# Half of the block sums of g moved from GpSimd instructions to adding DMAs, the first x in four loads, and a new written-out order

## The chip, the cores and the metric

The kernel runs on one core of a Trainium2 chip. The metric is the device time of one execution in microseconds (us). The kernel before takes 213.96 us, the median of three runs (213.93 to 214.35). Profiles come from one execution; its engines are TensorE (PE, with its weight loads listed apart as PEld), VectorE (DVE), ScalarE (ACT), GpSimd (POOL) and SyncE (SP, which here only issues DMAs). A queue named with a q (SPq, POOLq) is the sequencer of that engine.

## What is computed

Eight batches `b` of 8 heads, 512 tokens and 32 state rows, each of 64 elements. Tokens and state rows attend to each other, both with one shared score matrix, and the result goes through a two-layer network with a leaky rectifier:

```python
def _attn_ref(x, state):
    scores = scale * np.matmul(x, state.transpose(0, 1, 3, 2))
    a = softmax(scores)                      # over the 32 state rows
    xread = np.matmul(a, state)
    scores2 = scale * np.matmul(state, x.transpose(0, 1, 3, 2))
    a2 = softmax(scores2)                    # over the 512 tokens
    sread = np.matmul(a2, x)
    return np.concatenate([xread, sread], axis=2)

def _moe_ref(x, w_in, w_out, alpha):         # 4352 rows of 512; d_ff = 2048
    h = x @ w_in
    g = np.maximum(h, 0.0) + alpha * np.minimum(h, 0.0)
    return g @ w_out
```

## The kernel before

Every instruction is written out by hand in one string, `ORDER` (L18 to L99). A loop (L767) reads it token by token and calls the step that the token names, so the string fixes the order of the instructions on every engine and on every DMA queue. Each engine then works through its own instructions strictly in order, and waits where an operand is not there yet.

**The stages.** Since xread is `a @ state`, the first layer for the token rows is `a @ (state @ w_in)`. Steps `m` and `mo` make `m = state @ w_in` for batch b and quarter f of d_ff (PE, then a copy out of PSUM by ACT or DVE). The softmax over states is made by `sc` (scores, PE), `sb` (a 32 x 32 block transpose, DVE), `smax` (DVE), `ssh` (subtract, mostly POOL), `sexp` (ACT), `ssum` (DVE), `snorm` (multiply, POOL or DVE, L405) and `wb` (transpose back, DVE). Batch 0 takes a path of its own with smaller tiles: `cx` casts the loaded x, `xt` transposes it on PE, `xo` copies it out, `tsc` makes the scores, `at` and `ao` turn the weights. The softmax over tokens is `tm`, `nb`, `te`, `tsum`, `tn` and two DMA transposes (`xd` for x, `tt` for the weights); `rd` multiplies it with x on PE. The state rows of all batches are gathered and run through the network as a ninth, half-wide batch, b = 8.

**First layer.** `F.b.jc.k` is two matmuls of 512 columns (L556; four of 256 columns for b = 8, L565) into PSUM bank k, for one 128-row slice jc of d_ff. `N.b.jc` (ACT, L609) takes the negative part, `G.b.jc` (DVE, L612) adds it, times 1 - alpha, to h and writes the f16 tile g. `f`, `n` and `g` do the same for half of the tokens of batch 0.

**Second layer.** Batch 0 uses plain matmuls (`S`, L626). Batches 1 to 8 use a scheme with seven products of half-size blocks in place of eight. It needs four sums of blocks of w_out, made once (`W`, L670), and for each batch four sums of blocks of g (`U.b.i.c.e`, L683 to L694; i is the sum, c one half of it, e the engine). A block of g is (half of the tokens, half of d_ff), and all 64 sums are POOL instructions of 128 x 1024 f16 (128 x 512 for b = 8). Sum 2 reads sum 1, and sum 4 reads sum 2. `P.b.p.i.c` is product p: four matmuls of 256 columns (L715). Products 5, 6, 7 and 3 read sums 1, 2, 3 and 4. `K` copies a running product out of PSUM (L731), `Q` writes a quarter of the output: a sum or a copy into an `oq` tile, of which there are four, and a store issued by SP (L749).

**Loads.** The x of batch 0 comes in two loads of SP as f32 (L170) and is cast by DVE. All other loads (x of later batches L160, the states L203, w_in L212, w_out L218) are issued by POOL, which casts in the DMA. `Z.k.n` is a run of n idle matmuls that fill a wait of PE (L236). The small vector alpha comes in four loads of SP (L188) and is turned by `oma`.

Of the kernel before, what the change touches and what calls it, by code (L numbers as in the profile page):

```python
# [13 lines left out]
ALU = mybir.AluOpType  # L14
# [4 lines left out]
Z.0.3 stc.a stt.0 cx.0.1.v xt.0.0.1.1 xo.0.0.1.a wi.0 cx.0.0.v xt.0.0.0.2 xo.0.0.0.a sbd.0.v lst sbd.1.v Z.3.2 sto.a  # L19
Z.3.2 Z.3.3 cx.1.0.v xt.0.1.0.3 cx.1.1.v tsc.0.1.4 tsc.0.0 smax.0.0 ssh.v.0.0 xo.0.1.0.a xt.0.1.1.5 xo.0.1.1.a Z.1.3  # L20
Z.1.2 sc.0.0 sc.0.1 tsc.1.1.1 m.0.0.2.0 tsc.1.0 sexp.0.0 tm.0 smax.0.1 ssum.0.0 Z.3.3 mo.0.0.a.1 lx.1 Z.3.2 Z.3.2
Z.3.3 ssh.v.0.1 str.1.3 nb.0.a te.0.1 Z.5.3 str.0.5 Z.4.3 Z.4.3 te.0.0 sexp.0.1 Z.4.2 mo.0.0.v.0 Z.4.3 wi.1 ssum.0.1
wo.0 sro.0.a xt.1.0.0.4 snorm.p.0.0 at.0.0 ao.0.a wo.1 Z.1.3 tsum.0 snorm.p.0.1 xt.1.0.1.1 m.1.0 xt.1.1.0.2 sro.1.a
wi.2 oma.a xo.1.0.0.v wi.3 xo.1.0.1.v xo.1.1.0.a f.0.0.0.5 xt.1.1.1.0 n.0.0.0 mo.1.0.v at.1.4 ao.1.v m.0.1.1.3
tn.0.1.p mo.0.1.v.1 m.1.1 mo.1.1.a g.0.0.0.0 g.0.0.0.1 f.0.0.1.2 n.0.0.1 f.0.1.1.4 mo.0.1.a.0 n.0.1.1 f.0.1.0.3
xo.1.1.1.v g.0.0.1.1 g.0.0.1.0 sc.1 tm.1 m.2.0.5.0 mo.2.0.a.1 mo.2.0.a.0 F.0.5.1 N.0.5 F.0.4.2 N.0.4 nb.1.a te.1.1
g.0.1.1.0 g.0.1.1.1 G.0.5 S.0.3.0.0 wo.2 G.0.4 S.0.1.0.5 S.0.1.1 sb.1 F.0.7.4 N.0.7 G.0.7 F.0.6.1 wo.3 tn.0.0.p N.0.6
S.0.3.1 G.0.6 n.0.1.0 g.0.1.0.0 S.0.2.2.2 S.0.3.2 te.1.0 S.0.1.2 S.0.2.0 g.0.1.0.1 m.0.2 S.0.2.3 S.0.1.3 smax.1
mo.0.2.a F.0.8.4 N.0.8 G.0.8 W.1.1.p F.0.11.1 N.0.11 G.0.11 tsum.1 F.0.10.3 N.0.10 m.0.3 mo.0.3.a W.1.0.p lx.2 S.0.2.1
S.0.3.3 F.0.9.4 m.1.2 F.0.12.1 ssh.p.1 sexp.1 G.0.10 S.0.2.5 S.0.1.5 ssum.1.s N.0.9 G.0.9 F.0.13.3 S.0.3.5 mo.1.2.a  # L30
# [769 lines left out]
```

## Time and profile before

| What | us |
|---|---|
| median of three runs | 213.96 |
| the profiled execution | 214.07 |
| its span, first to last instruction | 212.0 |
| PE busy | 203.3 |
| POOL busy | 179.1 |
| DVE busy | 174.2 |
| ACT busy | 152.6 |
| the 64 sums of g on POOL (four groups of 16) | 128.0 |
| idle matmuls (L236) | 10.5 |

The profiled execution took 2.07 us more than its span; that part lies outside the instructions. Busy times overlap across engines. A PE that is busy all the time is one whose matmuls follow each other without a gap; the time from one matmul's start to the next is what it costs there, and less than the duration listed for one matmul, since matmuls are pipelined. The granted TensorE clock is full throughout.

### The profile page before, as it was taken

How to read it: one execution, taken by the hardware profiler on the slowest of the kernel's cores; microseconds unless marked ns; L12 is line 12 of the kernel's file. 1: busy time of each engine (PE TensorE's matmuls, PEld its weight loads, DVE VectorE, ACT ScalarE, POOL GpSimd, SP SyncE). 2: the span in 40 equal slices, each digit the busy share in tenths (PEclk: the TensorE clock that was granted, in tenths of full speed). 3: DMA queues.
4: the chain of work that ended last, by engine and by line, in shares of the span. 5: the costliest groups of instructions: out<-in, count | busy, mean ns of one | idle time of the engine just before them, and what ended most of it. 6: DMA issues, size and time to landing. Idle time of an engine off the chain costs nothing.

```text
span 212.0 us, 5108 instructions
## 1 busy us (share of the span) xinstructions
PE 203.3 (96%) x2034; PEld 137.7 (65%) x2034; DVE 174.2 (82%) x260; ACT 152.6 (72%) x300; POOL 179.1 (84%) x111
## 2 busy tenths in 40 slices
PE   7899999999999999999999998999999999999991
PEld 4556333444666665677667875667688777888880
DVE  0787988999999999999999999898999777654340
ACT  2577979999999999999797777887954584234100
POOL 8048848998999899999996999479996999999860
PEclk9999999999999999999999999999999999999999
DMA  6999995966665436778744539011521201111232
GB/s 159 219 204 207 206 204 89 160 165 90 152 105 89 106 84 135 110 134 143 183 117 49 103 106 192 3 51 40 162 53 49 99 3 49 49 53 49 74 124 102
DMA packets 43975, 23.70 MB, mean 112 GB/s; under 512 B 22192, under 2 KB 43440, under 8 KB 43952
## 3 DMA queue, kind: packets, MB, share of 16 engines
q1 hardware_dynamic: 31904, 15.22, 27.9%
q0 software_dynamic: 11776, 8.09, 26.6%
q8 instruction: 16, 0.26, 0.5%
q10 hardware_dynamic: 272, 0.07, 0.1%
q14 instruction: 7, 0.06, 0.1%
HBM read 17.31 MB, written 8.91 MB: 124 GB/s over the span
## 4 chain that ended last, share of the span: by engine, by line
PE 88%; DMA 7%; ACT 2%; issue 1%; SPq 0%; DVE 0%; ACTq 0%
PE h L556 25%; PE px L715 23%; PE pv L715 12%; PE o L626 6%; PE py L715 5%; PE m_ps L507 4%; PE h L565 3%; PE fill L236 3%; DMA xT<-xg 2%; DMA x<-in_x_dram 2%; PE sr_ps L480 2%; DMA out_dram<-oq 2%; DMA e2T<-e 1%; PE sc L314 1%; PE xT_ps L299 1%; PE h L578 1%
## 5 line engine op out<-in xcount | busy, mean ns | idle before, releaser
L612 DVE SCALAR_TENSOR_TENSOR g<-neg,oma_sb,h 128x512 f16<-128x512 f32 (+1 forms) x140 | 92.7, 708 | 11.6 <-ACT neg L609 11.1
L609 ACT ACTIVATE neg<-h 128x512 f32<-128x512 f32 (+1 forms) x140 | 75.0, 585 | 23.0 <-PE h L556 14.4
L556 PE MATMUL h<-aT,m 128*128 128x512 f16 x248 | 67.2, 379 | 0.1
L715 PEld LDWEIGHTS <-gsum 128*128 128x128 f16 x480 | 46.1, 98 | 16.8 <-issue 1.8
L715 PEld LDWEIGHTS <-g 128*128 128x128 f16 x360 | 35.0, 98 | 9.1 <-issue 0.9
L694 POOL TENSOR_TENSOR gsum<-g 128x1024 f16<-128x1024 f16 (+1 forms) x16 | 32.0, 2009 | 4.2 <-DVE g L612 3.6
L694 POOL TENSOR_TENSOR gsum<-g,g 128x1024 f16<-128x1024 f16 (+1 forms) x16 | 32.0, 2004 | 3.9 <-DVE g L612 3.8
L556 PEld LDWEIGHTS <-m 128*128 128x128 f16 x248 | 23.7, 98 | 15.5 <-issue 0.8
L694 POOL TENSOR_TENSOR gsum<-gsum,g 128x1024 f16<-128x1024 f16 (+1 forms) x16 | 32.1, 2006 | 1.1
L715 PE MATMUL px<-ws,gsum 128*128 128x256 f16 x240 | 32.6, 273 | 0.0
L694 POOL TENSOR_TENSOR gsum<-g,gsum 128x1024 f16<-128x1024 f16 (+1 forms) x16 | 31.9, 2005 | 0.1
L731 ACT COPY kept<-px 128x512 f32<-128x512 f32 (+1 forms) x22 | 12.7, 577 | 14.0 <-PE px L715 13.7
L533 ACT CAST m<-m_ps 128x512 f16<-128x512 f32 x36 | 20.0, 613 | 1.8 <-PE m_ps L507 1.5
L384 POOL TENSOR_TENSOR ts<-ts,mx 128x1024 f32<-128x1024 f32 x7 | 13.4, 1908 | 5.4 <-DVE mx L379 5.4
L715 PE MATMUL px<-w_out_sb,gsum 128*128 128x256 f16 x120 | 17.4, 273 | 0.0
L715 PE MATMUL pv<-ws,gsum 128*128 128x256 f16 x120 | 17.2, 273 | 0.0
L748 DVE TENSOR_TENSOR oq<-pv,kept 128x512 f32<-128x512 f32 (+1 forms) x16 | 10.5, 655 | 8.1 <-PE pv L715 6.7
L626 PE MATMUL o<-w_out_sb,g 128*128 128x512 f16 x64 | 17.1, 380 | 0.0
L715 PE MATMUL pv<-ws,g 128*128 128x256 f16 x120 | 16.9, 273 | 0.0
L715 PE MATMUL px<-w_out_sb,g 128*128 128x256 f16 x120 | 16.9, 273 | 0.0
L715 PE MATMUL py<-w_out_sb,g 128*128 128x256 f16 x120 | 16.2, 273 | 0.0
L531 ACT CAST m<-m_ps 128x1024 f16<-128x1024 f32 x12 | 12.4, 1032 | 1.3 <-PE m_ps L507 1.2
(76 smaller groups left out, 251.6 us busy)
## 6 DMA issues: line engine op xcount, KB each, us to landing
out_dram<-oq SPq DMA_DIRECT2D x28, 256.0 KB, 2.5
xg<-in_x_dram POOLq DMA_DIRECT2D x7, 512.0 KB, 6.9
w_in_sb<-in_moe_w_in_dram POOLq DMA_DIRECT2D x4, 512.0 KB, 9.3
w_out_sb<-in_moe_w_out_dram POOLq DMA_DIRECT2D x4, 512.0 KB, 12.2
x<-in_x_dram SPq DMA_DIRECT2D x2, 512.0 KB, 5.3
out_dram<-osb SPq DMA_DIRECT2D x4, 256.0 KB, 2.2
out_dram<-oq SPq DMA_DIRECT2D x4, 128.0 KB, 2.1
st<-in_state_dram POOLq DMA_DIRECT2D x1, 224.0 KB, 8.0
```

The source lines that it names most:

```text
L384: engine(e).tensor_tensor(blocks(cols(live["ts", b], j, S)), blocks(scored(b, j)), over_blocks(cols(live["mx", b], j, S // N)), ALU.subtract,)
L507: nc.tensor.matmul(t[N * k : N * (k + 1), :], st_head(b, h)[64 * r : 64 * r + 64, :], w_in_sb[64 * r : 64 * r + 64, c, 512 * f : 512 * (f ...
L531: copier(e)(m_tile(b, f), t)
L533: copier(e)(m_tile(b, f)[:, g, :], t[g])
L556: nc.tensor.matmul(h.rearrange("p (r j s) -> p r j s", r=2, j=2), ms[b, f][:, g, 128 * j : 128 * (j + 1)], weights(b, g), start=(g == 0), ...
L609: nc.scalar.activation(neg, h, RELU, bias=0.0, scale=-1.0)
L612: nc.vector.scalar_tensor_tensor(g_tile(b, jc), negs.pop((b, jc)), oma_sb[:, jc : jc + 1], hs.pop((b, jc)), ALU.mult, ALU.add,)
L626: nc.tensor.matmul(outs[b, q], g_tile(b, jc)[:, 128 * q : 128 * (q + 1)], w_out_sb[:, jc, :], start=not begun and jc == 2 * jc2, stop=left ...
L694: engine(e).tensor_tensor(t, x(), y(), op)
L715: nc.tensor.matmul(pbanks[b, name][:, i, :], of(b, c)[:, j, 128 * i : 128 * (i + 1)], moving[:, 4 * c + j, :], start=not begun and j == 0, ...
L731: copier(e)(t, pbanks[b, "x"])
L748: nc.vector.tensor_tensor(osb, pbanks[b, name], kept[b, add], ALU.add)
```

## The change

1. **Sums 3 and 4 of g** (`U.b.3` and `U.b.4`, 32 of the 64) carry the letter `d`: no POOL arithmetic, but a DMA issued by POOL that reads one block and adds it to another in place. Sum 3 then lies in the block (second half of the tokens, first half of d_ff), sum 4 in the block (first half of the tokens, second half of d_ff), and products 7 and 3 read them there. All four sums are plain additions now.
2. **Signs.** The sums of w_out's blocks are formed with other signs, and the kept products 2 and 4 are stored times -1.
3. **The first x** comes in four loads of half the size: two issued by SP, two by ACT, behind the load of the first states. The states of batches 1 to 7 come in two loads (`lst.0`, `lst.1`). The loads of alpha became a step (`la`) behind a memset on POOL; the memset of `st_pairs` went from DVE to POOL.
4. **The order** is written anew throughout, with engines chosen anew: of the six normalisations of states on DVE all are now on POOL, and more copies out of PSUM are on DVE and fewer on ACT. Batch 0's softmax over tokens and half of the later states' transposes are placed later. New arguments of `smax` and `ssum` are not used by the order.

The same matmuls are made as before, but for three idle ones fewer (55 against 58) and batch 0's slices 2 and 3 in two matmuls of 512 columns each in place of four of 256.

```diff
 ORDER = """
...
+wi.0 stc.a stt.0 sbd.0.a cx.0.0.v xt.0.0.0.1 cx.0.1.v xt.0.0.1.2 lst.0 cx.1.0.v la Z.3.6 sto.a xt.0.1.0.3 lx.1
+xo.0.0.0.a sbd.1.a wi.1 xo.0.0.1.v wi.2 wo.0 wi.3 tsc.0.0.4 tsc.0.1 smax.0.0 cx.1.1.a xt.0.1.1.5 wo.1 ssh.v.0.0
+xo.0.1.0.a xo.0.1.1.a Z.1.6 oma.a tsc.1.0.1 sexp.0.0 tsc.1.1 smax.0.1 Z.2.3 Z.2.6 str.0.2 ssh.v.0.1 sexp.0.1 m.0.0.0.3
+Z.5.9 sro.0.a ssum.0.0 m.1.0 mo.0.0.a.0 ssum.0.1 snorm.p.0.1 snorm.p.0.0 mo.0.0.v.1 mo.1.0.a xt.1.1.1.5 xo.1.1.1.v
+xt.1.0.0.4 xo.1.0.0.v xt.1.0.1.1 xt.1.1.0.2 at.1.0 m.2.0.3.5 xo.1.1.0.v wo.2 xo.1.0.1.a sc.1 at.0.4 ao.1.a mo.2.0.a.1
+ao.0.a f.0.0.1.1 m.0.1.2.0 mo.2.0.v.0 n.0.0.1 tm.1 nb.1.a sb.1 F.0.2.3 mo.0.1.a.0 Z.5.9 F.0.3.5 mo.0.1.v.1 g.0.0.1.0
...
+N.6.9 F.6.2.4 N.6.2 F.8.5.1 U.5.1.1.p Q.4.1.0 G.6.9 N.8.5 G.8.5 G.6.2 F.6.10.0 N.6.10 sexp.7 P.5.1.0.1.3 U.5.2.1.p
+P.5.1.1.0 G.6.10 ssum.7.s F.8.14.5 P.5.1.0.0 P.5.1.1.1 K.5.1.a F.6.0.2 U.5.3.1.d U.5.3.0.d F.6.7.1 F.8.0.4 U.5.2.0.p
+P.5.2.0.1.0 P.5.2.1.1 U.5.4.1.d N.6.7 G.6.7 P.5.2.1.0 N.6.0 G.6.0 P.5.2.0.0 Q.5.0.0 P.5.6.1.1 P.5.6.1.0 F.6.4.1 N.6.4
+F.6.1.2 N.6.1 P.5.6.0.0 P.5.6.0.1 N.8.14 G.6.4 N.8.0 F.6.12.0 K.5.2.v P.5.5.0.1 snorm.p.7 wb.7 G.8.0 P.5.5.1.1 G.6.1
+G.8.14 N.6.12 P.5.5.0.0 G.6.12 P.5.5.1.0 F.7.2.1 F.8.12.4 N.8.12 P.5.7.1.0.2 G.8.12 F.6.8.5 F.6.15.0 N.6.8 G.6.8
+P.5.7.0.0 F.8.8.4 N.8.8 G.8.8 P.5.7.1.1 N.6.15 P.5.7.0.1 K.5.4.v Q.5.1.1 F.6.11.5 N.6.11 F.6.14.4 U.5.4.0.d P.5.3.1.0
...
+P.8.6.0.0 P.7.4.1.0 Q.7.1.0 U.8.2.1.p P.8.6.0.1 P.7.3.1.0 P.8.7.0.1.5 K.8.2.v Q.7.0.1.v P.8.5.0.0 P.8.5.0.1 P.8.7.0.0
+K.8.4.v Q.8.1.1 P.6.3.0.1 P.6.3.0.0 P.8.4.0.1 Q.6.0.1.a P.8.4.0.0 P.8.3.0.0 Q.8.1.0 U.8.4.1.d P.8.3.0.1 Q.8.0.1.a
 """
...
-            nc.sync.dma_start(
-                t, x[0, :, 256 * j : 256 * (j + 1), :].rearrange("k (p r) d -> p k r d", r=2)
-            )
+            for g in range(2):
+                heads = slice(4 * g, 4 * g + 4)
+                (nc.scalar if j else nc.sync).dma_start(
+                    t[:, heads, :, :],
+                    x[0, heads, 256 * j : 256 * (j + 1), :].rearrange("k (p r) d -> p k r d", r=2),
+                )
...
-    nc.vector.memset(alpha_rows, 0.0)
-    for q in range(4):
-        nc.sync.dma_start(
...
+    def load_alpha():
+        nc.gpsimd.memset(alpha_rows, 0.0)
+        for q in range(4):
+            nc.sync.dma_start(
...
     W_SUMS = {
-        1: ((0, 1), (0, 0)),
-        3: ((1, 1), (0, 1)),
-        2: ((1, 1), 1),
-        4: ((1, 0), 2),
+        1: ((0, 0), (0, 1), ALU.subtract),
+        3: ((0, 1), (1, 1), ALU.subtract),
+        2: (3, (0, 0), ALU.subtract),
+        4: (2, (1, 0), ALU.add),
     }
...
     def g_sum(b, i, c, e):
         w = S // 2 if b < B else B * N // 2
+        x = {1: lambda: g_half(b, 1, 2 + c), 2: lambda: g_half(b, 0, c)}
+        x[3], x[4] = x[2], lambda: gss[b, 2, c]
+        y = {1: lambda: g_half(b, 1, c), 2: lambda: gss[b, 1, c]}
+        y[3], y[4] = y[1], lambda: g_half(b, 0, 2 + c)
+        if e == "d":
+            gss[b, i, c] = y[i]()
+            nc.gpsimd.dma_start(y[i](), x[i](), accum_op=ALU.add)
+            return
         t = gss[b, i, c] = moe.tile(
             [128, 4, w], F16, name=f"gsum_{b}_{i}_{c}", tag=f"gsum{i}{c}", bufs=1
         )
-        x, y, op = {
-            1: (lambda: g_half(b, 1, c), lambda: g_half(b, 1, 2 + c), ALU.add),
-            2: (lambda: gss[b, 1, c], lambda: g_half(b, 0, c), ALU.subtract),
-            3: (lambda: g_half(b, 0, c), lambda: g_half(b, 1, c), ALU.subtract),
-            4: (lambda: g_half(b, 0, 2 + c), lambda: gss[b, 2, c], ALU.subtract),
-        }[i]
-        engine(e).tensor_tensor(t, x(), y(), op)
+        engine(e).tensor_tensor(t, y[i](), x[i](), ALU.add)
...
-        copier(e)(t, pbanks[b, "x"])
+        if name == 1:
+            copier(e)(t, pbanks[b, "x"])
+        elif e == "a":
+            nc.scalar.mul(t, pbanks[b, "x"], -1.0)
+        else:
+            nc.vector.tensor_scalar_mul(t, pbanks[b, "x"], -1.0)
```

183 lines of the change are left out of this document (85 added, 98 removed).

## The prediction

> **What bounds the kernel now.** I read the page first, then the busy times by stretches, the list of waits, the groups by shape, the chain that ended last, and at last the timeline of both ends.
>
> ```profile
> span 212.0 us, 5108 instructions
> PE 203.3 (96%) x2034; PEld 137.7 (65%) x2034; DVE 174.2 (82%) x260; ACT 152.6 (72%) x300; POOL 179.1 (84%) x111
> PE   7899999999999999999999998999999999999991
> ```
>
> PE is the bound. The stretches say where it isn't full (columns: stretch, its length, busy us of PE, PEld, DVE, ACT, POOL):
>
> ```profile
> 0.00:20.00 20.00, 17.25 (x217) 11.37 (x218) 11.52 (x25) 11.03 (x22) 11.61 (x21) 1.00 1.11 197
> 20.00:35.00 15.00, 14.86 (x117) 5.92 (x115) 13.72 (x24) 13.66 (x26) 9.84 (x7) 1.00 1.13 180
> 35.00:60.00 25.00, 24.64 (x274) 12.88 (x266) 24.22 (x32) 23.75 (x48) 24.21 (x13) 1.00 0.70 128
> 60.00:130.00 70.00, 70.00 (x719) 47.92 (x718) 68.18 (x94) 62.88 (x124) 66.26 (x37) 1.00 0.61 120
> 130.00:133.00 3.00, 2.04 (x57) 1.46 (x63) 2.07 (x4) 1.29 (x3) 3.00 (x3) 1.00 0.60 125
> 133.00:203.00 70.00, 70.00 (x634) 54.51 (x631) 52.02 (x81) 39.29 (x81) 62.54 (x34) 1.00 0.18 58
> 203.00:207.60 4.60, 4.51 (x40) 3.65 (x38) 2.50 (x6) 0.37 (x1) 1.59 (x2) 1.00 0.41 145
> ```
>
> From 60 to 130 and 133 to 203 PE has no gap, at full clock. After 20 us its idle time is 0.14 + 0.36 + 0.96 + 0.09 = 1.55 us, whatever POOL does. The idle matmuls all lie before 20 us:
>
> ```profile
> 0.00:20.00 20.00, 10.50 (x58) 5.91 (x58) 1.00 1.11 197
> ```
>
> So of the first 20 us only 17.25 - 10.50 = 6.75 us is work that the result needs. Behind PE's last matmul 4.4 us follow. The change can win only in these three places: the start, the 1.55 us of gaps, the tail. POOL's 179 us are no bound; among the waits (us in total, times, longest) stands one on a sum of g:
>
> ```profile
> PEld L715 <- POOL gsum L694: 0.4, 1, 0.4
> ```
>
> **The change, part by part.** *The matmuls* that the result needs stay as they are: products and first-layer slices are counted alike in both orders (840 products' matmuls; 16 half-wide and 248 full ones become 8 and 252). In the saturated stages they cost what the chain of waits shows:
>
> ```profile
> 199.89 0.87 PE px L715 x8
> 144.14 0.86 PE h L556 x4
> 10.21 0.34 PE m_ps L507 x8
> 111.20 0.61 PE sr_ps L480 x32
> ```
>
> that is 0.436 us for a `P` token, 0.43 for an `F`, 0.34 for an `m`, 0.61 for an `rd`. Three fills fewer cost or save nothing by themselves: they stand in waits.
>
> *The sums.* 32 POOL instructions go, 28 of 2.13 us and four of 1.15, some 64 us of POOL; 32 DMA issues come. Prices:
>
> ```profile
> L694 POOL TENSOR_TENSOR gsum<-g,g x16: 1150/2125/2135, 50.8 to 199.9; 128x1024 f16<-128x1024 f16 x14, 128x512 f16<-128x512 f16 x2
> L406 DVE TENSOR_TENSOR an<-ts,r 128x1024 f16<-128x1024 f32 x6 | 7.3, 1219 | 0.0
> L406 POOL TENSOR_TENSOR an<-ts,r 128x1024 f16<-128x1024 f32 x1 | 1.9, 1912 | 1.0 <-DVE r L403 1.0
> L533 DVE CAST m<-m_ps 128x512 f16<-128x512 f32 x2 | 1.4, 684 | 0.0
> L212 POOL DMA_DIRECT2D w_in_sb<-in_moe_w_in_dram x4 | 3.3, 826 | 0.0
> L160 POOL DMA_DIRECT2D xg<-in_x_dram x4: 919/920/950, 59.4 to 112.7; - x4
> DMA to landing us min/median/max: 5.9/6.6/7.2
> out_dram<-oq SPq DMA_DIRECT2D x28, 256.0 KB, 2.5
> ```
>
> An issue by POOL takes 0.8 to 0.95 us; I take 0.92, since those issues fall into the same busy stages. That is 29 us, and the six normalisations that come over from DVE add 6 x 1.91 = 11.5 us, so POOL falls by some 23 us to about 156. PE waited for none of it, so all this is worth nothing by itself. What matters is the new delay: a sum on POOL was there 2.13 us after its start, a sum by DMA when it lands. No row shows an adding DMA. Bounds from the nearest rows, for 256 KB: below, SP's store of 256 KB, 2.5 us from issue to landing; above, POOL's loads of x, 512 KB each and cast on the way, at most 7.2 us, in case the adding doubles the traffic. I take 4.5 us, between the store of the same size and the load by the same engine. Both ends stay in the range.
>
> Is 4.5 us hidden? I laid the POOL queue against PE's order at the place that looks tightest, b = 5. Its last slice of g is F.5.13; from there to P.5.3.1.0, which reads sum 4, the new order holds on PE 23 `P`, 14 `F` of 512 columns and five of b = 8, two `m` and two `rd`: 10.0 + 6.0 + 2.2 + 0.7 + 1.2 = 20.1 us. On POOL, 2.4 us pass until g is there, an estimate from these two rows, 0.61 + 0.74 with about one instruction of queueing before each:
>
> ```profile
> L609 ACT ACTIVATE neg<-h 128x512 f32<-128x512 f32 x124 | 69.5, 610 | 14.8 <-PE h L556 14.4
> L612 DVE SCALAR_TENSOR_TENSOR g<-neg,oma_sb,h 128x512 f16<-128x512 f32 x124 | 85.7, 738 | 7.1 <-ACT neg L609 6.7
> ```
>
> Then come U.5.1.1, U.5.2.1, two issues, U.5.2.0, an issue and snorm.7: 3 x 2.13 + 3 x 0.92 + 1.91 = 11.1 us. U.5.4.0 is issued 13.5 us after F.5.13 and may take 20.1 - 13.5 = 6.6 us to land. In the same way U.1.3.0 has 8 us (14.9 of PE work less 2.4 + 2 x 2.13), and the last one, U.8.4.1, of half size, 13.5 (31 `P`) less 2.4 + 3 x 1.15 + 2 x 0.92 = 5.8 us. So a landing within some 5.8 to 6.6 us costs PE nothing. The other margin is the issue: P.5.6.1.0 comes 11.0 us after F.5.13 and needs U.5.2.0, on POOL 2.4 + 3 x 2.13 + 2 x 0.92 = 10.6 us after it. There is room for 0.4 us, so an issue of over 1.1 us would be felt.
>
> U.4 must also wait until PE has read its target in product 2. That puts whatever stands behind it on POOL (snorm, ssh, the next sum 1) behind PE; in b = 5 PE is through with P.5.2 10.6 us after F.5.13, before POOL comes to U.5.4.0 at 13.5. Zero, and if the cover goes, the same two margins shrink.
>
> *The engines' new shares.* Against 1.22 us times six off DVE stand eight copies of m (0.69) and ten kept products, so DVE stays near 175 us; ACT loses about 9. In 20 to 60 us DVE and ACT are both over 90% busy, and there a shift may open or close a gap; I count the 1.55 us of gaps as half closed, -0.8, with bounds of -1.5 and +1.5. The largest one is this:
>
> ```profile
> 126.41 2.79 SPq L291 DMA_TRANSPOSE xT<-xg  x1
> 129.30 1.28 SPq L465 DMA_TRANSPOSE e2T<-e  x1
> 132.29 0.68 PE L480 MATMUL sr_ps<-e2T,xg 128*64 128x32 f16 x32 [0.96 <-DMA e2T<-e]
> ```
>
> Here rd.5 waits for `tt.5`, which stood on SP behind `xd.7`. In the old order one `m` stands between `tt.5` and rd.5; in the new one 13 `P`, 8 `F` and an `m`, 9.5 us of PE work, so this gap should go.
>
> *The start* (timeline; the row of landings is that of alpha's loads).
>
> ```profile
> 0.74 1.12 SPq L170 DMA_DIRECT2D x<-in_x_dram  x2
> 1.90 2.89 SPq L188 DMA_DIRECT2D alpha_rows<-in_moe_alpha_dram  x4
> DMA to landing us min/median/max: 4.5/4.9/6.4
> 5.44 0.88 DVE L176 CAST xg<-x 128x512 f16<-128x512 f32 x2 [4.27 <-DMA x<-in_x_dram]
> 7.18 0.76 DVE L176 CAST xg<-x 128x512 f16<-128x512 f32 x2 [0.36 <-DMA x<-in_x_dram]
> 8.69 0.69 DVE L379 TENSOR_REDUCE mx<-tsc 128x16 f32<-128x512 f32 x1 [0.74 <-PE tsc L353]
> 14.95 0.20 DVE L272 STREAM_TRANSPOSE alpha_sb<-alpha_rows 128x32 f32<-128x32 f32 x1
> 18.12 0.60 PE L578 MATMUL h<-aT,m 128*128 128x256 f16 x4
> ```
>
> Four loads move the same bytes; two rings run side by side, so the first quarter may land at about 4.7 in place of 5.4, and the last near 7.1 as now. In the new order the first maximum still needs tsc.0.0, which stands behind cx.0.1 (second quarter), cx.1.0 and six fills: I get 8.7 us again. From there the chain of j = 1 (a shift, 0.2 for alpha, maximum, shift and two sums on DVE, each about as long as the maximum, one normalisation on POOL, then transposes of x and scores of b = 1 on PE) brings the first h to about 17 us against 18.1. But less of the rest is done by then: half of the later states' transposes and batch 0's token scores stand later. Counted as work needed, both orders have some 6.5 us done at 20 us. I take a gain of 0.2 us, with bounds of -1.5 and +1.5. Alpha is now read on DVE at about 10 us, not 14.95. Its loads wait for a memset that stands on POOL behind two issues, so they go out from about 4 to 5.7 us and land 4.9 us later, at 9 to 10.6: I take no wait, and leave half a microsecond to the bounds.
>
> *The tail* (chain, then timeline):
>
> ```profile
> 204.43 3.57 DMA out_dram<-oq
> 208.18 0.37 ACT oq L746
> 206.91 0.60 PE L715 MATMUL px<-w_out_sb,gsum 128*128 128x256 f16 x4
> ```
>
> PE ends at 207.51, and the last copy starts at 208.18 since it waited for one of four `oq` tiles to be stored. In the new order the store that it waits for, Q.7.0.1, is copied after P.7.3.1.0, with ten `P` (4.4 us) still to come; copy 0.69, then 2.5 to 3.6 to land: it is there in time. Gain 0.6 us, bounds 0 and 0.65.
>
> Sum: -0.2 - 0.8 - 0.6 + 0 = -1.6 us. The profiled execution took 214.07 (212.0 of span and 2.07 around it), 0.11 over the median of 213.96. From the median: 212.4 us.
>
> **Rivals.** *The sums land late (slower).* If an adding DMA takes 8.5 us, U.5.4.0 is 1.9 late and U.8.4.1 (5 to 6 us at half size) is near its limit; the batches 1 to 7 each lose what is over their own margin of 6.6 to 8 us, 0.5 to 1.9, together some 7 us: 212.4 + 7 = 219; at 7.2 us about 2 us: 214.4. An issue of 1.5 us instead of 0.92 gives 2 x 0.58 - 0.4 = 0.8 us in each of seven batches, 5.6 us: 218. It decides from 1.6 us lost in all. For it: nothing in the trace shows the operation. Against it: POOL's issues in the saturated stages took 0.92 to 0.95, as at the start. Chance 0.25.
>
> The Trainium skill has a rule that speaks for this rival, on the page "SBUF — State Buffer", section "SBUF: two separate sides": while VectorE runs in a two-port mode, GpSimd can't write the descriptors of the DMAs it issues. By that rule issues would stretch by up to a DVE instruction each, and the time would be the 218 of this rival; the issues of x at 0.92 to 0.95 us beside a DVE that is 97% busy don't show it.
>
> *The start gets worse (slower).* DVE takes alpha between the two halves of batch 0's softmax. If the last of alpha's loads takes the longest landing seen, 6.4 us, it is there at 5.7 + 6.4 = 12.1, DVE stands still for 2 us and so does the chain behind it: 212.4 + 2 = 214.4. It decides from 1.6 us. Against it: the median of the four is 4.9. Chance 0.10.
>
> *Nothing to measure.* The gaps closed reappear elsewhere, since in 20 to 60 us PE, DVE and ACT are all above 90%: -0.6 for the tail, + 0.5: 213.9. Chance 0.13.
>
> **How the numbers follow.** 0.52 for the forecast, at 212.4, its own range 210.3 (start 1.5 better, all gaps closed) to 213.5. A measurement of this kernel tells about 0.2%, 0.43 us, from no change. Faster 0.52, same 0.13, slower 0.25 + 0.10 = 0.35. The range leaves out a tenth above (the late sums at their worst) and less below: 210.3 to 217.5.
>
> **What would show it.** Right: PE without gaps from about 20 us; no matmul of products 7 and 3 waiting for a DMA; POOL near 156 us; adding DMAs that land within 6 us, issues below 1.1; the last copy starting with PE's end; DVE not waiting for alpha. Wrong: idle PE in front of L715 named after a DMA into g or after a sum, once a batch; POOL's issues well over 1 us; a first h after 18 us.

## The result, and the profile after

The changed kernel takes 223.1 us (median of four runs, 221.8 to 224.0), the kernel before, beside it on the same chip, 213.95 (213.9 to 214.4). The ratio is 1.042, with a 95% interval of 1.036 to 1.048. The forecast of 212.4 us was on the wrong side; the time is also above the upper end of the range, 217.5. Ratios leave out executions that took over 1.5% longer than the fastest of the same kernel at a lower mean clock: one of run e3 below (226.85 us, clock 0.981) and two of run e4 (254.33, which is the one profiled, and 255.41).

The profiled execution, the longest of the four, took 224.03 us. From its page: span, engines, the slices of PE and of its clock, then POOL's DMA queue (packets, MB, share).

```profile
span 222.0 us, 5117 instructions
PE 205.9 (93%) x2027; PEld 137.4 (62%) x2027; DVE 174.9 (79%) x263; ACT 147.0 (66%) x285; POOL 172.0 (77%) x122
PE   7699969979999999999989999999999989969991
PEclk9999999979999999999999999999999999999998
q0 software_dynamic: 28688, 15.96, 56.9%
```

PE is still the longest engine, but it now has gaps after 20 us. POOL fell from 179 us to 172, not to 156. The waits of PE after the change (us in total, times, longest):

```profile
PE px L724 <- POOL gsum L703: 3.2, 4, 1.7
PE h L563 <- DVE g L619: 2.2, 2, 1.9
PE sr_ps L487 <- DMA e2T<-e: 1.7, 1, 1.7
PE px L724 <- DMA g<-gsum: 0.7, 1, 0.7
```

Before, the first two and the last were not there. To see where the time went, compare two places that every kernel passes: PE's first matmul of a product, and its last. Of before, the first (the last, 206.91 + 0.60, stands in the prediction); then both of after:

```profile
52.06 1.04 PE L715 MATMUL px<-w_out_sb,g 128*128 128x256 f16 x8
```

```profile
57.76 0.61 PE L724 MATMUL px<-w_out_sb,g 128*128 128x256 f16 x4
...
217.61 0.61 PE L724 MATMUL px<-w_out_sb,g 128*128 128x256 f16 x4 [0.72 <-DMA g<-gsum]
```

So the products begin 57.76 - 52.06 = 5.7 us later, though the first adding DMA goes out only at 61.2 us. From the first product to the end of the last one it takes 160.46 us instead of 155.45, 5.0 more. Behind the last product stand 222.0 - 218.22 = 3.8 us instead of 4.5, 0.7 less. Sum: 5.7 + 5.0 - 0.7 = 10.0, the difference of the spans. The two orders don't stand alike at the first product, though: the new one has done three `m` and an `rd` more by then (14 and 2 against 11 and 1), at the prediction's prices 3 x 0.34 + 0.61 = 1.6 us. So of the 5.7 us some 4.1 are lost, and behind the first product 5.0 + 1.6 = 6.6. There are thus two losses, and the smaller one lies ahead of the first product.

*The early loss.* The stretches of after that answer to those of before:

```profile
0.00:20.00 20.00, 16.74 (x188) 11.26 (x189) 12.11 (x23) 12.98 (x26) 12.12 (x22) 1.00 1.13 198
20.00:35.00 15.00, 12.91 (x116) 5.07 (x114) 14.47 (x21) 13.21 (x25) 10.92 (x7) 1.00 1.12 179
35.00:60.00 25.00, 23.35 (x248) 10.37 (x247) 19.03 (x30) 20.76 (x40) 17.56 (x13) 0.93 0.64 117
46.90:50.20 3.30, 3.30 (x9) 1.19 (x8) 2.17 (x3) 2.77 (x9) 2.71 (x2) 0.51 0.56 61
```

By 20 us PE has done more of the needed work than before, 16.74 busy less 8.84 of idle matmuls = 7.9 us instead of 6.75. Then it idles 2.1 us between 20 and 35 us and 1.65 us between 35 and 60 (before, 0.14 and 0.36), and for 3.3 us it runs at half the clock. The timeline of SP and PE there shows the second pause:

```profile
37.97 0.38 SPq L652 DMA_DIRECT2D out_dram<-osb  x1
38.53 2.11 SPq L298 DMA_TRANSPOSE xT<-xg  x1
40.73 1.70 SPq L472 DMA_TRANSPOSE e2T<-e  x1
```

```profile
43.70 0.40 PE L321 MATMUL sc<-xT,stT 64*32 64x256 f16 x16
45.76 0.68 PE L487 MATMUL sr_ps<-e2T,xg 128*64 128x32 f16 x32 [1.65 <-DMA e2T<-e]
46.37 2.42 PE L563 MATMUL h<-aT,m 128*128 128x512 f16 x6
```

`rd.0` waits for `tt.0`, which stands on SP behind the store of O.0.1 and `xd.2`. In the old order no store stood ahead of the two transposes, and SP issued `tt.0` 3.5 us earlier:

```profile
37.21 1.63 SPq L465 DMA_TRANSPOSE e2T<-e  x1
```

PE came to rd.0 there at 43.65, 6.4 us after that issue; in the new order it was free 3.4 us after it (45.76 - 1.65 - 40.73). PE's work between the two tokens is much the same in both orders, at the prediction's prices (an `S` taken like an `F`) 3.8 us before and 4.2 after; what differs is the store ahead of them. Like the gap at rd.5, it is a transpose that stands behind other work on SP.

*The late loss.* POOL's issues in the groups of after (busy, mean ns, idle before), their landing in us, then a stretch of POOL's timeline:

```profile
L698 POOL DMA_DIRECT2D g<-gsum x16 | 25.3, 1736 | 2.1 <-POOL gsum L703 1.8 <-DVE g L619 0.3
L698 POOL DMA_DIRECT2D g<-g x16 | 20.9, 1334 | 2.5 <-POOL gsum L703 2.5
```

```profile
g<-g POOLq DMA_DIRECT2D x14, 256.0 KB, 5.0
g<-gsum POOLq DMA_DIRECT2D x14, 256.0 KB, 5.5
```

```profile
191.77 1.29 POOL L698 DMA_DIRECT2D g<-gsum  x1 [0.30 <-POOL gsum L703]
192.59 2.63 POOL L703 TENSOR_TENSOR gsum<-g,g 128x1024 f16<-128x1024 f16 x1
195.52 1.29 POOL L698 DMA_DIRECT2D g<-g  x1 [0.30 <-POOL gsum L703]
196.34 2.62 POOL L703 TENSOR_TENSOR gsum<-gsum,g 128x1024 f16<-128x1024 f16 x1
```

An adding DMA's issue takes at least 1.29 us. The instruction behind it starts 0.82 us after the issue did, beside the rest of it, but takes 2.62 us instead of 2.13. And POOL waits 0.30 us for its own sum before each issue. From 192.59 + 2.63 = 195.22, the end of one sum, to 196.34 + 2.62 = 198.96, the end of the next, 3.74 us pass, of which 2.13 would be the sum alone: an adding DMA costs POOL 1.6 us there, where 0.92 was forecast. PE waits for late sums in the batches 3, 4, 6 and 7 (0.56, 0.34, 0.59 and 1.72 us), and not in b = 5, where the prediction had looked.

### The profile page after: what moved, and what is told of

It reads as the page before. It is cut to its first block, busy times and chain, and to the rows that moved or that the text cites. A ratio compares the mean times of both kernels' runs of the same rounds, so it can differ in the third digit from the quotient of the medians.

```text
span 222.0 us, 5117 instructions
## 1 busy us (share of the span) xinstructions
PE 205.9 (93%) x2027; PEld 137.4 (62%) x2027; DVE 174.9 (79%) x263; ACT 147.0 (66%) x285; POOL 172.0 (77%) x122
## 3 DMA queue, kind: packets, MB, share of 16 engines
q0 software_dynamic: 28688, 15.96, 56.9%
## 4 chain that ended last, share of the span: by engine, by line
POOL 36%; PE 22%; DVE 17%; issue 10%; DMA 7%; ACT 5%; ACTq 1%; POOLq 0%; DVEq 0%
POOL gsum L703 18%; DVE g L619 7%; POOL g L698 7%; PE h L563 5%; PE px L724 5%; PE o L633 4%; POOL an L413 4%; POOL ts L391 3%; DMA x<-in_x_dram 3%; POOL ws L677 3%; DMA e2T<-e 2%; DMA out_dram<-oq 2%; PE pv L724 2%; PE fill L243 2%; PE m_ps L514 2%
## 5 line engine op out<-in xcount | busy, mean ns | idle before, releaser
L724 PEld LDWEIGHTS <-g 128*128 128x128 f16 x600 | 58.3, 98 | 17.6 <-issue 1.4
L703 POOL TENSOR_TENSOR gsum<-gsum,g 128x1024 f16<-128x1024 f16 (+1 forms) x16 | 37.2, 2322 | 0.5
L724 PE MATMUL pv<-ws,g 128*128 128x256 f16 x240 | 33.4, 273 | 0.2 <-DVE oq L762 0.2
L724 PE MATMUL px<-w_out_sb,g 128*128 128x256 f16 x240 | 32.4, 273 | 0.7 <-DMA g<-gsum 0.7
L724 PEld LDWEIGHTS <-gsum 128*128 128x128 f16 x240 | 22.9, 98 | 13.1 <-POOL gsum L703 4.7
L413 POOL TENSOR_TENSOR an<-ts,r 128x1024 f16<-128x1024 f32 (+1 forms) x9 | 18.2, 2031 | 12.0 <-DVE r L410 10.0
L698 POOL DMA_DIRECT2D g<-gsum x16 | 25.3, 1736 | 2.1 <-POOL gsum L703 1.8
L698 POOL DMA_DIRECT2D g<-g x16 | 20.9, 1334 | 2.5 <-POOL gsum L703 2.5
L161 POOL DMA_DIRECT2D xg<-in_x_dram x7 | 8.9, 1271 | 3.9 <-PE sr_ps L487 3.9
L514 PE MATMUL m_ps<-w_in_sb,stT 64*32 64x512 f16 x256 | 11.7, 384 | 0.0
```

The source lines that it names most:

```text
L413: engine(e).tensor_tensor(blocks(cols(live["an", b], j, S)), blocks(cols(live["ts", b], j, S)), over_blocks(cols(live["r1", b], j, S // N) ...
L514: nc.tensor.matmul(t[N * k : N * (k + 1), :], st_head(b, h)[64 * r : 64 * r + 64, :], w_in_sb[64 * r : 64 * r + 64, c, 512 * f : 512 * (f ...
L698: nc.gpsimd.dma_start(y[i](), x[i](), accum_op=ALU.add)
L703: engine(e).tensor_tensor(t, y[i](), x[i](), ALU.add)
L724: nc.tensor.matmul(pbanks[b, name][:, i, :], of(b, c)[:, j, 128 * i : 128 * (i + 1)], moving[:, 4 * c + j, :], start=not begun and j == 0, ...
```

## The experiments

Runs are compared by their ratio to the kernel before, which ran beside them on the same chip (214.0 to 214.35 us). "Stage" below means the time from the first product's matmul to the end of the last one's, read as above. Among the orders that come from the new one the stage holds the same work. It is compared, and not the span, because the first 50 us of this start vary by themselves (last section). Each stage comes from one profile.

**No adds at all (e1).**

```diff
-            nc.gpsimd.dma_start(y[i](), x[i](), accum_op=ALU.add)
```

> The changed kernel with the line left out that issues the adding DMAs: the tokens U.b.3.c.d and U.b.4.c.d do nothing. Sums 3 and 4 of g are not formed, their products read the plain halves of g instead, so the output is wrong; PE, DVE, ACT and the rest of POOL do all their work in the same order. It tells what the adds cost in all (issue by POOL, landing, waits of POOL before an issue) from what the new order costs without them. Theory A (the slowdown has two parts: some 4.6 us lost between 27 and 51 us, ahead of the first adding DMA at 61 us, by the new order of the early stage, and some 5 us lost after 61 us by the adds): 223.1 - 5 = 218, POOL 172 - 46 - some 15 for the shorter instructions beside the issues = 110 to 125 us, the waits of PE for a sum of POOL gone, the two stalls at 29.6 and 43.8 us and the half clock behind them still there. Rival B (all of it is the adds): 214 or less. Rival C (all of it is the order): 223.

Measured: 216.2 us, ratio 1.0105 (1.0061 to 1.0149). The waits at 29 and 45 us are there as before, and the sums of POOL are back at 2.13 us. The products begin at 56.22, and the stage takes 154.27 us, 6.2 less than after. So the adds cost some 6 us, and the new order without them is still a little slower than before: neither rival holds. The half clock was expected and is missing: in this profile the same pause of 1.70 us isn't followed by it. (Of the four executions one had a mean clock of 0.992 and took 218.04 us, the others 0.996 to 1.000 and at most 216.3.)

**The pause at 44 us (e3).**

```diff
-... O.0.1.a tn.0.1.p F.1.14.3 F.1.12.2 xd.2 ... tn.0.0.p ... tt.0 S.0.3.7 ...
+... tn.0.1.p tn.0.0.p tt.0 xd.2 O.0.1.a F.1.14.3 F.1.12.2 ...
```

> The changed kernel with four tokens moved ahead in the order, tn.0.1.p tn.0.0.p tt.0 xd.2, to right before O.0.1.a, so that on SP the transposing DMA of batch 0's scores goes out before the store of O.0.1 and the load of xd.2. Nothing is left out. Theory A (rd.0 waited 1.7 us on PE for this DMA, and the half clock of 3.4 us that begins 2 us later follows from that pause): both go, 223.1 - 1.7 - 1.7 = 219.7; the granted clock of 47 to 50 us at 1.00. Rival A3 (the pause goes, but the half clock is due to something else, such as PE's load): 221.4, with the half clock still there. Rival A4 (POOL and ACT are late there anyway, so that PE only waits elsewhere): 222.5 to 223.5.

Measured: ratio 1.0287 (1.0254 to 1.0319), that is 220.4 us, 2.8 less than after. PE has no pause at rd.0 and is full from 35 to 60 us, at full clock:

```profile
43.32 0.68 PE L487 MATMUL sr_ps<-e2T,xg 128*64 128x32 f16 x32
43.93 1.47 PE L563 MATMUL h<-aT,m 128*128 128x512 f16 x6
```

```profile
35.00:60.00 25.00, 25.00 (x287) 12.23 (x286) 22.17 (x32) 23.98 (x46) 20.92 (x14) 1.00 0.87 145
```

The products begin at 53.63, 4.1 us earlier than in after; the stage, 160.68, is 0.2 longer. Four tokens on SP's queue make 2.8 us. Theory A holds for the pause. That the half clock follows from it fits, but isn't shown: the clock is full in this profile, but it was also full behind the pause in e1. The theory's sum (3.4) was a little high, since the half clock isn't in every run of after: two of its four runs had a mean clock of 0.990 and took 223.6 and 224.0 us, two had 0.998 and took 221.8 and 222.7. By these pairs the half clock is worth about 1.5 us in the runs that have it.

**The new order without adds and without the pause (g1).** e3's order, and the line of the first experiment left out.

> The run e3_sp_order with the line left out that issues the adding DMAs (sums 3 and 4 are not formed, so the output is wrong); the clean base for the price of the adds, without the pause at 44 us and without the half clock. Theory A (the adds cost 5 us, all after 61 us): 220.4 - 5.1 = 215.3, less if the first loads land as early as in the profile of e3. Rival B (without the pause other losses open in the early stage): 216 as in e1_no_adds.

Measured: 214.13 us, ratio 0.9989 (0.9975 to 1.0003): no difference from before, and lower than both forecasts (215.3 and 216). Its queue, first and last product:

```profile
q0 software_dynamic: 11792, 8.09, 25.9%
```

```profile
53.95 0.61 PE L723 MATMUL px<-w_out_sb,g 128*128 128x256 f16 x4
...
207.19 1.04 PE L723 MATMUL px<-w_out_sb,g 128*128 128x256 f16 x8
```

The stage takes 154.28 us, 1.2 less than before. So the account by ratios is closed: pause and half clock 1.3% (1.0419 to 1.0287), adds 3.0% (1.0287 to 0.9989), rest nothing. The 1.9 us by which the products begin later than before and the 1.2 us by which the stage is shorter are for the most part the three `m` and the `rd` that stand ahead of the first product; with them put back (1.6 us) 0.3 us are lost ahead of it and 0.4 in the stage, and 0.4 are gained behind it.

**Copies in place of adds (e2).** What does the adding itself cost? The order is that of after, with the pause.

```diff
-            nc.gpsimd.dma_start(y[i](), x[i](), accum_op=ALU.add)
+            nc.gpsimd.dma_start(y[i](), x[i]())
```

> The changed kernel with the 32 DMAs as plain copies from one half of g to the other, still issued by POOL, without the adding. Products 3 and 4 then multiply copies in place of sums, so the output is wrong; instructions, waits and places are the same. It tells the adding (a longer landing, more traffic) from the issue. Theory A1 (what costs after 61 us is the issue by POOL: 1.3 us instead of the 0.92 predicted, and the POOL instruction behind it 0.5 us longer, so that the sums made by POOL come late): same as the changed kernel, 222.5 to 223.5, the sums of POOL behind an issue again at 2.6 us, the landing at 2.5 to 4.5 us. Rival A2 (the adding costs, in landing or in the time of the issue): 219 to 221, issues at 0.92 us.

Measured: 217.55 us, ratio 1.0146 (1.0115 to 1.0178), by the ratios only 0.9 us above the kernel without any; the stage takes 154.9, 0.6 more. Theory A1 as written is wrong: it is not the issue as such. Rival A2 is right that the adding costs, though the time is below its 219 to 221 too. Queue, issues (min/median/max in ns) and landing of these copies, and the sum behind an issue:

```profile
q0 software_dynamic: 14224, 15.96, 39.1%
L698 POOL DMA_DIRECT2D g<-g x16: 747/767/829, 59.9 to 199.8; - x16
g<-g POOLq DMA_DIRECT2D x14, 256.0 KB, 3.4
```

```profile
183.66 0.76 POOL L698 DMA_DIRECT2D g<-g  x1 [0.29 <-POOL gsum L703]
184.45 2.14 POOL L703 TENSOR_TENSOR gsum<-gsum,g 128x1024 f16<-128x1024 f16 x1
```

A copy by POOL is issued in 0.77 us, doesn't slow the next instruction, and lands in 3.4 us. With the adding it is 1.29 us or more, 0.5 us on the next instruction, and 5.0 to 5.5 us. The queue shows what goes with it: without any of these DMAs it has 11,792 packets, with copies 14,224, with adds 28,688. On average over the 32, a copy goes in some 76 packets, an add in some 528, though the bytes are the same.

**Adds that nobody waits for (f1, g2).** Two runs point the adding DMAs at scratch, in e3's order, so that POOL issues them and no product reads them. In the first the scratch is contiguous, in the second it has the 512 B rows of g. Both also clear the scratch at the start, with some 2 us of memsets on DVE.

```diff
-            nc.gpsimd.dma_start(y[i](), x[i](), accum_op=ALU.add)
+            s = scratch[len(done) % len(scratch)]
+            done.append(s)
+            nc.gpsimd.dma_start(s[:, :, :w], x[i](), accum_op=ALU.add)
```

> The changed kernel with tt.0 and xd.2 ahead on SP as in the run e3_sp_order, and with each of the 32 adding DMAs pointed at one of four scratch tiles that nobody reads, in place of the half of g. POOL issues the same adding DMAs at the same places and they move as much, but no product waits for a landing; sums 3 and 4 are not formed, so the output is wrong. To be held against e3_sp_order (220.4), which differs only in the target, and against the run without adds less the 2.6 us that e3 gained (216.2 - 2.6 = 213.6). Theory A (POOL's own time is what costs: an adding issue lasts 1.3 to 1.7 us, the instruction behind it 0.3 to 0.5 us longer, and sums 1 and 2 come late): 219.4 to 220.4, with the PE waits for POOL gsum of 3 to 5 us. Rival B (the landing of 5 to 5.5 us is what costs): 213.6 to 214.6, without these waits.

> As f1_scratch (adding DMAs into scratch that nobody reads, so the output is wrong, tt.0 and xd.2 ahead on SP), but the scratch is laid out in the rows of 512 B that the halves of g have, so that each DMA has as many packets as in the changed kernel; f1_scratch had a third fewer. To be held against g1_e3_no_adds (no adds) and e3_sp_order (adds into g, 220.4). Theory A (POOL's time for these packets is most of the 5 us, and f1_scratch was cheaper for its fewer packets): 218.5 to 220. Rival B (it is the landing that products, and POOL behind them, wait for; f1_scratch's 1.5 us is all that POOL's time costs): 216.5 to 217.5.

Measured: contiguous 216.9 us, ratio 1.0144 (1.0117 to 1.0172), between the two forecasts; with rows 218.5 us, ratio 1.0203 (1.0172 to 1.0235), at theory A's lower end. The queue of the first, then the wait for POOL and the first and last product of the second, which has as many packets as after (28,688):

```profile
q0 software_dynamic: 23312, 15.96, 54.5%
```

```profile
PEld L731 <- POOL gsum L710: 2.6, 4, 1.3
55.00 0.61 PE L731 MATMUL px<-w_out_sb,g 128*128 128x256 f16 x4
...
211.50 1.04 PE L731 MATMUL px<-w_out_sb,g 128*128 128x256 f16 x8
```

The stages make a ladder (packets of one DMA worked out as above, from 11,792):

| kernel | packets | stage, us | over no adds |
|---|---|---|---|
| no adds (g1) | 0 | 154.3 | |
| copies, awaited (e2) | 76 | 154.9 | 0.6 |
| adds to contiguous scratch (f1) | 360 | 155.8 | 1.5 |
| adds to scratch in rows (g2) | 528 | 157.5 | 3.3 |
| adds to g, awaited (e3) | 528 | 160.7 | 6.4 |

Half of what the adds cost is POOL's time, and that goes up with the packets. The other half comes in when the target is g. PE's weight loads show where both are lost; in e3:

```profile
PEld L724 <- POOL gsum L703: 4.7, 5, 2.0
PEld L724 <- DMA g<-gsum: 1.3, 1, 1.3
```

For late sums they wait 0.2 us in g1, 0.4 in e2, 1.8 in f1, 2.6 in g2 and 4.7 in e3, for a landing only in e3. So of the 3.1 us between g2 and e3 some 2.1 are sums that come later still, and some 1.3 the landing in front of the last product. Why the sums come later is in part argued: POOL waits 0.30 us or a little more ahead of a DMA for its own sum, 13 times in e3 and after. Ahead of 6 of these the sum is the DMA's source, and g2 has them too; ahead of the other 7 it is sum 1, which reads the target, and g2 lacks these.

It is not the adding as such that makes an issue dear. In f1 sum 2, a source in one run per partition, is added to a target that is laid out alike; three such DMAs, at 129.20, 185.40 and 192.16 us, were issued in 0.89 us each, where g2, with short rows in the target alone, shows 1.29 at the same three places. So the cost goes with the packets, and the adds of the change, between short rows, have the most.

**POOL's own sums in the new order (f2).** 30 of the 32 adds made by POOL again (`.d` to `.p`), in e3's order.

```diff
-... U.2.3.1.d ... U.4.4.0.d ...
+... U.2.3.1.p ... U.4.4.0.p ...
```

> The changed kernel with tt.0 and xd.2 ahead on SP as in e3_sp_order, and with 30 of the 32 adding DMAs made by POOL itself again as sums into tiles of their own, at the same places (U.7.3.0, U.7.3.1 and U.8.4.0 stand up to 14 tokens later, since these tiles must come free; U.6.4 stays with the DMA). Nothing is left out. It tells what the DMA form gains or loses against POOL's own sum, in the new order. Theory A (a sum costs POOL 2.13 us, an adding DMA 1.3 to 1.7 us for the issue, 0.3 of waiting and 0.4 for the slower instruction behind it, so 2.0 to 2.4 us: nothing is gained): within 2 us of e3_sp_order, 218.5 to 222.5, with POOL at 130 + 62 = 190 us. Rival B (the form is a gain, since POOL has 20 us less to do, and only the room for the landing lacks): 223 to 228, POOL saturated from 60 us on and PE waiting for sums in every batch.

Measured: 231.85 us, ratio 1.0844 (1.0814 to 1.0874). Rival B holds in its mechanism, and the time is above its 223 to 228: POOL is busy for 190.7 us, and PE waits for sums all along.

```profile
PEld L724 <- POOL gsum L703: 12.3, 8, 2.7
```

So in *this* order the DMA form is a gain, of 11 us. A likely reason, which no run separates, is that this order has put the normalisations on POOL and left little room for sums. The DMA form is dear only against an order where POOL makes the sums and nobody waits.

**The adds in the old order (e4).** 28 adds, five of them later in the order than the sums were, w_out's signs to suit, everything else as before.

```diff
-... U.1.3.0.p U.1.3.1.p ... U.1.4.0.p ...
+... U.1.3.0.d U.1.3.1.d ... U.1.4.0.d ...
```

> The kernel before, in its own order and with its own start, with 28 of the 32 sums 3 and 4 as adding DMAs issued by POOL at the place of the sum (moved behind sum 1 where the target is still to be read), and with the signs of w_out that go with it; U.2.4 and U.7.4 stay sums of POOL. Nothing is left out. It has the adds alone. Theory A1 (28 issues of 1.3 us and 0.5 us on the next POOL instruction against 28 sums of 2 us saved: POOL is no fuller than before, but sums 1 and 2 that stand behind issues come late, and a landing of 5 to 5.5 us is longer than the 2.1 us of a sum for which the old order has room): 214 + 2 to 6 = 216 to 220, with PE waits for DMA g<-g or g<-gsum among the gaps. Rival (the adds are free where POOL is the only one that gains, as the prediction took it): 213.5 to 214.5.

Measured: ratio 1.168 (1.159 to 1.178), some 36 us lost, far outside both forecasts. The products begin on time (52.04), but then wait for landings, and POOL stands in front of issues whose target PE still reads:

```profile
PE pv L719 <- DMA g<-g: 11.1, 5, 3.5
PE sr_ps L482 <- DMA e2T<-e: 9.6, 1, 9.6
L693 POOL DMA_DIRECT2D g<-gsum x12 | 21.4, 1957 | 9.2 <-PE py L719 5.3 <-PE h L558 3.9
```

So adds put into an order that was made for sums cost far more than in the new one. The one wait of 9.6 us for a transposing DMA stays unexplained.

**The signs alone (e6).** The old order with the new signs, all sums on POOL.

```diff
-        1: ((0, 1), (0, 0)),
+        1: ((0, 0), (0, 1), ALU.subtract),
```

> The kernel before in its own order, with nothing of the change but w_out's signs: the eight differences of w_out formed anew (1 = 00 - 01, 3 = 01 - 11, 2 = 3 - 00, 4 = 2 + 10) and all sums of g formed by adding, all on POOL. Nothing is left out. Every theory: the same as before, 213.6 to 214.4; anything else would mean that the signs or the code of the sums cost by themselves, and that e4_adds_old does not show the adds alone.

Measured: 214.16 us, ratio 1.0002 (0.9977 to 1.0027). The signs cost nothing.

**Two moves that failed (f3, g3).** First DVE's order, to close PE's wait of 1.9 us at 29 us:

```diff
-... tm.0 S.0.3.3 F.0.13.2 N.0.13 ssum.1.s F.0.12.3 nb.0.a te.0.0 te.0.1 S.0.1.3 G.0.13 G.0.14 ...
+... S.0.3.3 F.0.13.2 N.0.13 F.0.12.3 S.0.1.3 G.0.13 G.0.14 tm.0 ssum.1.s nb.0.a te.0.0 te.0.1 ...
```

> The run e3_sp_order with one more move: on DVE G.0.13 and G.0.14 stand ahead of tm.0 and ssum.1 (with nb.0.a, te.0.0 and te.0.1 behind tm.0), so that the bank of PSUM that PE waits for at 29 us comes free 2.4 us earlier. Nothing is left out. Theory A (PE's 1.9 us there is a wait in the order of DVE): 220.4 - 1.6 = 218.8, PE full from 27 to 31 us. Rival B (DVE and ACT are both over 90% busy in this stage, so that the wait reappears before 36 us): 220 to 220.6.

Measured: 225.2 us, ratio 1.0532 (1.0494 to 1.0570), 5 us worse than e3. The wait at 29 us shrinks to 0.6, but two others take its place, and the half clock is back behind the second (six matmuls of 512 columns in 2.74 us, which took 1.47 in e3):

```profile
34.54 0.41 PE L514 MATMUL m_ps<-w_in_sb,stT 64*32 64x512 f16 x8 [1.62 <-ACT e L450]
...
47.52 0.63 PE L321 MATMUL sc<-xT,stT 64*32 64x256 f16 x16 [2.86 <-DMA xT<-xg]
...
49.05 2.74 PE L563 MATMUL h<-aT,m 128*128 128x512 f16 x6
```

Batch 0's scores are now late, and `xd.2` stands on SP behind their transposition. Rival B was right that the wait moves, but not that this is free.

Second, five normalisations back on DVE (`snorm.p` to `snorm.v` for batches 3 to 7):

> The run e3_sp_order with the normalisations of batches 3 to 7 back on DVE (snorm.v in place of snorm.p, five of the six that the change moved to POOL). Nothing is left out. It takes 5 x 2.3 = 11.5 us off POOL and puts 5 x 1.2 = 6 us on DVE. Theory A (sums come late since POOL has too much to do in 60 to 200 us): 220.4 - 3 = 217.4, with the waits of PE for POOL gsum of 3.2 us halved. Rival B (a late sum is late by its own chain, an adding issue of 1.3 to 1.7 us ahead of it and the landing behind it, or DVE now holds up g): 219.5 to 221.5.

Measured: 230.4 us, ratio 1.0730 (1.0683 to 1.0777), 10 us worse and far above both forecasts. The waits for sums do shrink (PE for POOL gsum from 3.2 to 2.3 us), but DVE is nearly full from 60 us on (14.96 of 15 us), and behind it PE waits for g (5.0 us in all, on two lines), the transposed attention weights (2.5) and a transposed x (2.6):

```profile
60.00:75.00 15.00, 15.00 (x173) 9.74 (x171) 14.96 (x24) 13.23 (x26) 14.69 (x9) 1.00 1.23 175
75.00:110.00 35.00, 28.23 (x259) 18.73 (x257) 31.20 (x37) 23.26 (x49) 26.36 (x15) 0.95 0.90 146
```

**A small gain (f4).** The kernel before with two of the new order's gains.

```diff
-... P.4.6.0.0 xd.7 N.5.7 ... P.4.5.1.0 tt.5 m.7.1.1.2 rd.5.4 ...
+... P.4.6.0.0 tt.5 xd.7 N.5.7 ... P.4.5.1.0 m.7.1.1.2 rd.5.4 ...
-... P.7.3.1.1 P.8.7.0.0.5 ... Q.7.0.1.v ...
+... P.7.3.1.1 Q.7.0.1.v P.8.7.0.0.5 ...
```

> The kernel before, with all sums on POOL and its own start, and with two of the new order's gains alone: tt.5 stands ahead of xd.7 on SP, and Q.7.0.1 right behind P.7.3.1.1, 3 us earlier, so that the tile of the last store is free. Nothing is left out. Theory A (the new order's gains at the gap before rd.5, 0.96 us, and at the last copy, 0.6 us, are to be had without the adds): 214.2 - 1.5 = 212.7. Rival B (the gap at rd.5 moves to the transposed x that now goes out second): 213.6.

Measured: 213.47 us against 214.01, ratio 0.9981 (0.9966 to 0.9996). That is a gain of 0.2%, barely clear of the noise and a third of what theory A gave; rival B's 213.6 is nearer. The two places:

```profile
131.13 0.68 PE L480 MATMUL sr_ps<-e2T,xg 128*64 128x32 f16 x32
132.39 0.41 PE L314 MATMUL sc<-xT,stT 64*32 64x256 f16 x16 [0.58 <-DMA xT<-xg]
...
207.75 0.37 ACT L746 COPY oq<-px 128x256 f32<-128x256 f32 x1 [3.04 <-DMA out_dram<-oq]
```

rd.5 no longer waits, but the scores behind it wait 0.58 us for the transposed x that goes out second: of 0.96 us, 0.4 are left as a gain. The last copy waits as long as before. The copy that its store depends on begins at 203.13 instead of 203.72, but so does all around it (PE's last matmul at 206.32 instead of 206.91): nothing else stands on DVE between the old place of Q.7.0.1 and the new one, so that move left DVE's order as it was and tested nothing.

## Why the prediction was wrong

Its first reading held: PE bounds both kernels, it had no gap worth the name before, and so a fuller or emptier POOL was worth nothing by itself. The step that followed, that the adds are covered and that the new order opens no gaps, did not. The larger loss, 6.4 us by the stages of e3 and g1, is in the first term below, the smaller, some 4.1 us, in the fourth. By its own terms:

- *The issue on POOL, 0.92 us, bounds 0.8 to 0.95.* This is the step that failed first. It was taken from plain loads by the same engine. An adding DMA's issue is 1.29 us or more, and it adds 0.5 us to the instruction behind it and 0.30 us of waiting ahead of it, 1.6 us in all in the stretch shown. The copies (0.77 us) show that the nearest row was right for a plain DMA; what it left out is that an add between short rows goes in seven times the packets. The text had said that an issue of over 1.1 us would be felt; it was. The rival with the dear issue (1.5 us, 5.6 us lost, 218 in all) was right that sums 1 and 2 would come late behind the issues. That its size is near the 6.4 us which the adds cost is in part luck: it had 0.8 us in each of seven batches, while PE waited 0.3 to 0.6 us in three and 1.7 in one, and half of the cost came only with g as the target. Its chance of 0.25 was too low, given that no row bore on the operation.
- *POOL at 156 us.* It is 172. Without the adds POOL is busy 130.1 us (e1), where the forecast's terms give some 127; so the adds are 42 us in place of 29, the same price, and 3 us lie elsewhere.
- *The landing, 4.5 us, bounds 2.5 to 7.2.* Measured 5.0 and 5.5 as the medians of the two kinds, inside the bounds and inside the margins of 5.8 to 6.6; the longest took 8.3. As forecast no matmul of products 7 waits for one; only the last product waits, 0.72 us, for U.8.4.1, which landed some 5.4 us after its issue began (217.61 - 212.22), within the 5.8 that it had been given. The margin was smaller than worked out: from the end of U.8.1.0 (203.11) to its issue (212.22) 9.1 us passed, where three sums and three issues at the forecast's prices make 6.2. And the place laid out as the tightest, b = 5, is one where PE doesn't wait.
- *Gaps half closed, -0.8, bounds -1.5 to +1.5.* This is the step that failed second. The gap at rd.5 went, as worked out. But no wait between SP's queue and PE was looked for at rd.0, where the new order opens one of 1.65 us. The check made for rd.5, how much PE work lies between a `tt` and its `rd`, would hardly have found it (4.2 us, where the old order has 3.8); the store that stands ahead of `tt.0` on SP shows it. With the half clock behind it (some 1.5 us when it occurs) and the wait of 1.9 us for DVE at 29 us, the stages in front of the products lost some 4.1 us. The bound of +1.5 had no row behind it; it was worked out from gaps that were there, not from those that could open.
- *The start, -0.2, bounds -1.5 to +1.5.* First h at 16.42 instead of 18.12 and the first maximum at 7.70 instead of 8.69: somewhat better than forecast, with 7.9 us of needed work done at 20 us where some 6.5 was forecast. The last quarter landed at 8.51, not at 7.1. DVE waits 0.98 us for alpha, which was given no wait.
- *The tail, -0.6.* Measured -0.7: the last copy starts with PE's end, as forecast. That is in part luck: here PE's last product comes late by its own wait of 0.72 us, and in g1, without the adds, the last copy waits for a store again and the tail is only 0.4 us shorter than before.
- *The Trainium skill's rule* from "SBUF — State Buffer", section "SBUF: two separate sides", that DVE can keep GpSimd from writing descriptors, would have given the same 218. The runs show no sign of it: the copies' issues lie between 747 and 829 ns beside a DVE that is 81% busy. What lengthens an issue here goes with the number of packets (0.89 us against 1.29 in f1 and g2).

## What to carry to other kernels

Price an operation that no row shows by the whole of what its engine does for it, with the instructions beside and behind it, and give it a chance that fits not knowing: here a DMA that adds between short rows took seven times the packets of one that copies. When an order is written anew, check every wait between queues, not only the one that the change closes; one transposing DMA behind a store and another transpose cost 2.8 us. An engine that is off the critical path is still worth nothing when emptied, and work that is moved off it may only fit an order that was made around it.

## What the runs showed of the hardware

- A DMA that adds to its target, in rows of 512 B, goes in about 528 packets on average, a copy between the same tiles in about 76. Its issue by POOL takes at least 1.29 us, the copy's 0.77; the sum behind it takes 2.62 instead of 2.13, and 256 KB land in 5.0 to 5.5 instead of 3.4 us (medians). With a source and a target in one run per partition the issue of an add took 0.89 us (f1). The Trainium skill, page "DMA: Bandwidth & Descriptors", section "Anatomy of one DMA — SWDGE (gpsimd) path", calls the making of descriptors a small cost, of which one can emit a lot before it shows. For the copies these runs agree; for the adds they don't.
- The clock fell to half for 3.3 us behind a pause of PE of 1.65 us, in the profile of after, and not behind the same pause of 1.70 us in the first experiment. The Trainium skill, page "TensorE: Matmul & The Clock Gate", section "What's actually happening", has a gate that watches free-running windows of some 3.4 us and halves the clock after an idle one. The length and the chance in it agree; but PE idled for half of such a window only, with short matmuls on both sides. If the pause set it off, which e3's full clock without the pause makes likely, under 2 us can be enough. It isn't shown to be the only cause: one execution of e3 had a mean clock of 0.981.
- The last quarter of x's first load, the second on ACT's queue, landed between 7.69 and 9.15 us in ten profiles of the same start, while the first on SP's queue stayed within 4.05 to 4.42. PE's transposes waited for its cast between 0.2 us (the earliest) and 2.3 us (the latest). Such a spread in the start is why the stages were compared, not the spans.
